# Gate and value products contracted over 32 inducing points in four row groups of TensorE, with a new token layout, load path and output path

## The chip, the cores and the metric

One core of one Trainium2 chip. The metric is device time in microseconds of one execution. Every kernel below was run next to the kernel before on the same chip. The kernel before scatters over 2.8% (1162 to 1195 us in all) at an unchanged mean TensorE clock of 0.985 to 0.995; runs over 1.5% above the fastest count as slow and are left out of the ratios. The **granted clock** is the share of TensorE's full clock that the profile's records show; in these runs it is 1.0 or 0.5 at any one time.

## The reference, cut to what matters

```python
B, N, m, C = 4, 12416, 32, 128            # x: (B, N, C), inducing: (m, C)
def mab(q, kv):                            # softmax attention, keys = values
    s = scale * (q @ kv.T);  s -= s.max(-1)
    a = exp(s);  a /= a.sum(-1) + 1e-9
    return a @ kv
h = mab(inducing, x)                       # "phase 1": 32 rows for each batch
z = mab(x, h)                              # 49664 tokens x 128
gate, val = relu(z @ w_gate), z @ w_val    # 128 -> 1536, each
out = (gate * val) @ w_out                 # 1536 -> 128
```

Each token's z is a mix of only 32 rows of h. So z @ w_gate = a @ (h @ w_gate), with h @ w_gate having 32 rows. The sum that divides the softmax can come out of the relu and out of the product. It then divides twice, at the very end.

## The kernel before

It works in blocks of 512 tokens, 24.25 blocks to a batch. `s2` is the score product of a block, `p2` its exponential, `zt` the block's z. The scores are [32 x 512], and z is made from them. Then come 12 feature tiles of 128, with a gate product, a value product, a relu on ScalarE, a multiply on VectorE and an output product each.

```python
for b in range(B):
    nc.gpsimd.dma_start(out=xh[b], in_=x[b])            # fp32 -> fp16 copy of x in DRAM
    for q in range(4):
        nc.sync.dma_start_transpose(out=xT[:, rows], in_=xh[b][rows])
    nc.sync.dma_start(out=x_sb[:, :, 0:C], in_=xh[b]...)
    ...                                                  # phase 1: s1, exp, h
    def stage_zt(j):
        nc.tensor.matmul(zT_ps, h16, p2[:, cols])        # z of the block
        nc.scalar.copy(out=zt, in_=zT_ps)
        ...                                              # z2c, reciprocal, its square
    def stage_ffn(G, ...):
        for i in range(NFF):                             # 12 feature tiles
            nc.tensor.matmul(g_ps, wg[:, i], zt)         # 128 rows contracted
            nc.tensor.matmul(v_ps, wv[:, i], zt)
            nc.scalar.activation(out=g16, in_=g_ps, func=AF.Relu, bias=zbias, scale=1.0)
            nc.vector.tensor_tensor(out=gv[:, i], in0=g16, in1=v_ps, op=ALU.mult)
            ...                                          # four tiles later:
            nc.tensor.matmul(outT_ps, wo[:, k], gv[:, k], start=(k == 0), ...)
        nc.scalar.copy(out=oT16, in_=outT_ps)
    ...   # later: 4 transposes on TensorE, 4 scalings on VectorE, store
```

PSUM is split by hand: 1 + 1 + 2 + 3 + 1 banks of 128 x 512 fp32.

The softmax here doesn't subtract the row's maximum and nothing guards it: scores larger than these inputs give would overflow.

## Time and profile before

| | before |
|---|---|
| time (3 runs) | 1177.48 us median, 1170.03 to 1189.86 |
| first gate product | 190.8 us |
| one block of 512 tokens | 9.47 us, of which TensorE needs 9.23 |

The page of the kernel before: its first line (busy us, share of the span, instructions), the granted TensorE clock in 40 slices of 29.4 us, the chain that ended last by engine, and two groups. A group line gives busy us and the mean ns of one, then the idle time before them with what ended most of it.

```profile
PE 986.6 (84%) x5357; PEld 426.7 (36%) x5357; DVE 844.2 (72%) x1803; ACT 913.0 (78%) x1606; POOL 5.0 (0%) x13
...
PEclk9999998999999999999999989999999999999999
...
PE 81%; SPq 12%; DMA 3%; ACT 2%; DVE 1%; issue 1%; POOL 0%; DVEq 0%; ACTq 0%; POOLq 0%
...
L273 DVE TENSOR_TENSOR gv<-g,v_ps 128x512 f16<-128x512 f16 (+1 forms) x1200 | 748.8, 665 | 94.9 <-PE v_ps L258 82.1
L266 ACT ACTIVATE g<-g_ps,zbias 128x512 f16<-128x512 f32 (+1 forms) x1200 | 742.5, 672 | 45.9 <-PE g_ps L251 39.9
```

The chain is TensorE for 81% and the SP queue for 12%. The latter is the transposing DMA that waits at the start. ScalarE hardly appears in the chain although its relus take 742 us: it keeps up. The waits of VectorE and ScalarE end with a product of TensorE.

### The profile page before, as it was taken

What the parts mean: (1) busy time and instruction counts of PE and PEld (TensorE: products, weight loads), DVE (VectorE), ACT (ScalarE), POOL (GpSimd) and SP (SyncE); (2) the same over time, 40 slices, a digit from 0 to 9 for tenths busy, and PEclk for the clock granted to TensorE, in tenths of its full rate; (3) what the DMA queues carried; (4) which work ended last, traced back from release to release, by engine and by line L of the source; (5) the groups of instructions that cost most, each with busy time, mean ns of one, the idle gap of its engine ahead of it and who ended that gap; (6) DMA issues with size and microseconds to landing.
All of it is one profiled execution on the core that took longest, in us unless ns stands there. A gap on an engine that the chain in (4) does not pass through costs nothing.

```text
span 1177.6 us, 16537 instructions
## 1 busy us (share of the span) xinstructions
PE 986.6 (84%) x5357; PEld 426.7 (36%) x5357; DVE 844.2 (72%) x1803; ACT 913.0 (78%) x1606; POOL 5.0 (0%) x13
## 2 busy tenths in 40 slices
PE   0000018999999999999999999999999999999998
PEld 0000014444444453444444444444444534444443
DVE  0000003999998948989999849998989489999987
ACT  0000025999999979999999879999999799999997
POOL 1000000000000000000000000000000000000000
PEclk9999998999999999999999989999999999999999
DMA  9999999000001443000000650011000000000001
GB/s 160 102 94 75 57 196 215 26 28 28 28 30 35 95 109 80 28 28 28 28 28 28 145 120 19 28 32 32 28 28 28 30 10 28 28 28 28 28 28 48
DMA packets 116472, 65.83 MB, mean 56 GB/s; under 512 B 53505, under 2 KB 115617, under 8 KB 115873
## 3 DMA queue, kind: packets, MB, share of 16 engines
q1 hardware_dynamic: 113968, 50.88, 25.3%
q0 software_dynamic: 2416, 13.89, 8.8%
q8 instruction: 42, 0.69, 0.3%
q14 instruction: 46, 0.37, 0.1%
HBM read 40.52 MB, written 38.14 MB: 67 GB/s over the span
## 4 chain that ended last, share of the span: by engine, by line
PE 81%; SPq 12%; DMA 3%; ACT 2%; DVE 1%; issue 1%; POOL 0%; DVEq 0%; ACTq 0%; POOLq 0%
PE g_ps L251 26%; PE v_ps L258 21%; PE outT_ps L287 14%; SPq L101 12%; PE outT_ps L295 7%; PE s_ps L165 3%; PE zT_ps L181 3%; PE h_ps L138 2%; PE z2c_ps L187 2%; PE ot_ps L216 2%; ACT g L266 2%; DMA xh_stage<-in_x_dram 1%; DMA x_sb<-xh_stage 1%; DVE gv L273 1%; PE s_psg L122 1%
## 5 line engine op out<-in xcount | busy, mean ns | idle before, releaser
L273 DVE TENSOR_TENSOR gv<-g,v_ps 128x512 f16<-128x512 f16 (+1 forms) x1200 | 748.8, 665 | 94.9 <-PE v_ps L258 82.1
L266 ACT ACTIVATE g<-g_ps,zbias 128x512 f16<-128x512 f32 (+1 forms) x1200 | 742.5, 672 | 45.9 <-PE g_ps L251 39.9
L258 PE MATMUL v_ps<-zt,wv 128*128 128x512 f16 (+1 forms) x1200 | 434.6, 376 | 0.3
L251 PE MATMUL g_ps<-zt,wg 128*128 128x512 f16 (+1 forms) x1200 | 426.9, 378 | 1.8
L287 PE MATMUL outT_ps<-gv,wo 128*128 128x512 f16 (+1 forms) x800 | 283.6, 374 | 0.8
L258 PEld LDWEIGHTS <-wv 128*128 128x128 f16 x1200 | 117.9, 98 | 103.6 <-issue 13.0
L251 PEld LDWEIGHTS <-wg 128*128 128x128 f16 x1200 | 106.5, 98 | 119.9 <-issue 43.1
L295 PE MATMUL outT_ps<-gv,wo 128*128 128x512 f16 (+1 forms) x400 | 148.1, 372 | 0.0
L146 DVE RECIPROCAL z1i<-h_ps 32x1 f32<-32x1 f32 x4 | 0.6, 156 | 205.3 <-PE h_ps L138 205.3
L122 PE MATMUL s_psg<-indT,xT 128*128 128x32 f16 x196 | 13.6, 181 | 156.0 <-DMA xT<-xh_stage 154.9
L129 ACT ACTIVATE p1T<-s_psg,zbias 128x128 f16<-128x128 f32 (+1 forms) x52 | 18.8, 367 | 161.1 <-PE s_psg L122 160.5
L217 DVE TENSOR_SCALAR osb<-ot_ps,z2isq 128x128 f32<-128x128 f16 x388 | 134.0, 345 | 10.8 <-PE ot_ps L216 8.8
L287 PEld LDWEIGHTS <-wo 128*128 128x128 f16 x800 | 77.9, 98 | 91.5 <-issue 4.2
L216 PE MATMUL ot_ps<-eye,oT 128*128 128x128 f16 x388 | 84.8, 219 | 1.4 <-DVE osb L217 1.3
L168 ACT ACTIVATE p<-s_ps,zbias 32x512 f16<-32x512 f32 (+1 forms) x100 | 66.3, 663 | 14.6 <-PE s_ps L165 4.6
L122 PEld LDWEIGHTS <-xT 128*128 128x128 f16 x388 | 16.0, 98 | 164.1 <-DMA xT<-xh_stage 157.3
L183 ACT CAST zt<-zT_ps 128x512 f16<-128x512 f32 (+1 forms) x100 | 58.3, 583 | 1.1 <-PE zT_ps L181 1.1
L216 PEld LDWEIGHTS <-oT 128*128 128x128 f16 x388 | 37.7, 97 | 56.4 <-issue 23.2
L303 ACT CAST oT<-outT_ps 128x512 f16<-128x512 f32 (+1 forms) x100 | 56.5, 565 | 0.9 <-PE outT_ps L295 0.9
L295 PEld LDWEIGHTS <-wo 128*128 128x128 f16 x400 | 38.9, 97 | 47.9 <-issue 12.9
L165 PE MATMUL s_ps<-xT,hT 128*32 128x512 f16 (+1 forms) x100 | 39.9, 399 | 5.4 <-ACT p L168 4.3
L138 PE MATMUL h_ps<-x_sb,p1T 128*32 128x129 f16 x388 | 32.4, 228 | 14.1 <-DMA x_sb<-xh_stage 14.1
(32 smaller groups left out, 213.0 us busy)
## 6 DMA issues: line engine op xcount, KB each, us to landing
out_dram<-osb SPq DMA_DIRECT2D x96, 256.0 KB, 2.3
xh_stage<-in_x_dram POOLq DMA_DIRECT2D x4, 3104.0 KB, 126.3
wg<-in_moe_w_gate_dram POOLq DMA_DIRECT2D x1, 384.0 KB, 18.6
wv<-in_moe_w_val_dram POOLq DMA_DIRECT2D x1, 384.0 KB, 19.9
wo<-in_moe_w_out_dram POOLq DMA_DIRECT2D x1, 384.0 KB, 107.1
xT<-xh_stage SPq DMA_TRANSPOSE x16, 6.2
out_dram<-osb SPq DMA_DIRECT2D x4, 64.0 KB, 1.7
x_sb<-xh_stage SPq DMA_DIRECT2D x4, 0.2 KB, 16.6
```

The source lines that it names most:

```text
L101: nc.sync.dma_start_transpose(out=xT[:, rows], in_=xh[b][rows])
L165: nc.tensor.matmul(s2_ps[:M, 0:BW], hT[:, 0:M], xT[:, cols], start=True, stop=True)
L168: nc.scalar.activation(out=p2[:, cols], in_=s2_ps[:M, 0:BW], func=AF.Exp, bias=zbias[:M], scale=sm_scale,)
L183: nc.scalar.copy(out=zt[:, 0:BW], in_=zT_ps[:, 0:BW])
L216: nc.tensor.transpose(dst, oT16[:, jj * P : (jj + 1) * P], eye)
L217: nc.vector.tensor_scalar(out=osb[:, jj, :], in0=dst, scalar1=z2isqs[j][:, jj : jj + 1], scalar2=None, op0=ALU.mult,)
L251: nc.tensor.matmul(g_ps[:, 0:BW], wg[:, i * P : (i + 1) * P], zt[:, 0:BW], start=True, stop=True,)
L258: nc.tensor.matmul(v_ps[:, 0:BW], wv[:, i * P : (i + 1) * P], zt[:, 0:BW], start=True, stop=True,)
L266: nc.scalar.activation(out=g16[:, 0:BW], in_=g_ps[:, 0:BW], func=AF.Relu, bias=zbias, scale=1.0,)
L273: nc.vector.tensor_tensor(out=gv[:, i, 0:BW], in0=g16[:, 0:BW], in1=v_ps[:, 0:BW], op=ALU.mult,)
L287: nc.tensor.matmul(outT_ps[:, 0:BW], wo[:, k, :], gv[:, k, 0:BW], start=(k == 0), stop=False,)
L295: nc.tensor.matmul(outT_ps[:, 0:BW], wo[:, k, :], gv[:, k, 0:BW], start=False, stop=(k == NFF - 1),)
```

## The change

The intent: take z out. Per batch, h @ w_gate and h @ w_val are computed once (`hgv`, laid out as four copies of 32 rows: gate, value, gate, value). The scores of two blocks are laid out in the same four groups of 32 partitions. The four products of a feature tile for two blocks then contract over 32 rows each, and each reads another 32 partitions, called a row group of the array below. Further: x is loaded as fp32 straight to SBUF with 97 neighbouring tokens to a partition; phase 1 of the next batch is spread over the present one; the output is transposed by DMA and scaled on GpSimd; all PSUM tiles come from one ring of eight banks; the order of instructions is written by hand.

```diff
-    ps_g = lambda s, d, n: ps("pG", 2, s, d, n)      (and four more pools)
+    def ring(name, shape=None, dtype=FP32):
+        return psum.tile(shape or [P, BLK], dtype, tag="ring", bufs=8, name=name)
...
-        nc.gpsimd.dma_start(out=xh[b], in_=x[b])
+    xv = [x[b].rearrange("(p t) c -> p t c", p=P) for b in range(B)]
+        nc.sync.dma_start(out=x32, in_=xv[b][:, t0:t1, :])
...
+                nc.tensor.matmul(ps[64 * k : 64 * k + 64, :], hT, xTs(xT, t0, TPB), ...)   # s2, k = 0, 1
+            nc.scalar.activation(out=p2, in_=ps, func=AF.Exp, scale=sm_scale)
...
-                nc.tensor.matmul(g_ps[:, 0:BW], wg[:, i * P : (i + 1) * P], zt[:, 0:BW], ...)
-                nc.tensor.matmul(v_ps[:, 0:BW], wv[:, i * P : (i + 1) * P], zt[:, 0:BW], ...)
-                nc.scalar.activation(out=g16[:, 0:BW], in_=g_ps[:, 0:BW], func=AF.Relu, bias=zbias, scale=1.0)
+                    for k in range(2):
+                        for j in range(2):
+                            ps = ring("gv_ps")
+                            r = 64 * k + 32 * j
+                            nc.tensor.matmul(ps, hgv[r : r + 32, s * P : (s + 1) * P], p2[r : r + 32, :], ...)
+                for f in fill.pop(at, []):       # s2, z2, s1 or h of another pair, by a table of slots
+                    f()
+                out_work(at, 2.0 if full else 1.0)   # two output products
+                for k in range(len(pss) // 2):
+                    nc.scalar.activation(out=g16, in_=pss[2 * k], func=AF.Relu)
+                    nc.vector.tensor_tensor(out=dst, in0=g16, in1=pss[2 * k + 1], op=ALU.mult)
+                    if k == 0:
+                        for f in todo:           # exps, casts, DMA issues, by the same table
+                            f()
...
+                ev_s2(b, pr, base + 6)           # s2 of the next pair goes into slot 6
+            def s1(q=q, at=at + 18): ...         # s1 of the next batch: slot 6 as well (18 = 12 + 6)
+                fill[at + 18].append(s1)
...
-                        nc.tensor.transpose(dst, oT16[:, jj * P : (jj + 1) * P], eye)
-                        nc.vector.tensor_scalar(out=osb[:, jj, :], in0=dst, scalar1=z2isqs[j]..., op0=ALU.mult)
+                nc.sync.dma_start_transpose(out=o16[:, 0:nt, :], in_=oT[:, 0:w])
+                        nc.gpsimd.tensor_scalar(out=osb[:, t, :], in0=o16[:, t, :], scalar1=zz, scalar2=zz,
+                                                op0=ALU.mult, op1=ALU.mult)
```

A **slot** below is a pair of blocks times one feature tile: four products, two relus, two multiplies, two output products. A pair has 12 slots, numbered 0 to 11.

## The prediction

> **What bounds the kernel now.** I read the page first (engine shares, the 40 slices), then the chain of work in order of time, then the timelines of TensorE, ScalarE and VectorE over one block of the steady part. The page's slices:
>
> ```profile
> PE   0000018999999999999999999999999999999998
> DVE  0000003999998948989999849998989489999987
> ACT  0000025999999979999999879999999799999997
> ```
>
> Each digit stands for 29.4 us. The reader is to see three things: six empty slices ahead, a dip at three places in the middle, and for the rest all three engines near full. So there are three separate accounts: the start, the three batch boundaries, the steady part. The start, from the chain in order of time:
>
> ```profile
> 1.26 17.64 DMA xh_stage<-in_x_dram
> 18.91 131.35 SPq L101
> ...
> 162.35 17.03 DMA x_sb<-xh_stage
> 179.42 7.07 PE h_ps L138 x97
> ...
> 190.79 0.54 PE g_ps L251
> ```
>
> The first batch of x is in DRAM as fp16 after 18.9 us, but its transposing DMA (L101) then sits in the queue for 131 us, behind the staging of the other batches and the weights; then x_sb is read, then h. The first gate product starts at 190.8 us. Nothing of that start is arithmetic. The steady part, from ScalarE's timeline (two exps of s2, L168, lie two blocks of 512 tokens apart):
>
> ```profile
> 362.83 0.68 ACT L168 ACTIVATE p<-s_ps,zbias 32x512 f16<-32x512 f32 x1
> 363.41 1.81 ACT L266 ACTIVATE g<-g_ps,zbias 128x512 f16<-128x512 f32 x3
> 365.12 0.58 ACT L303 CAST oT<-outT_ps 128x512 f16<-128x512 f32 x1
> 365.59 0.60 ACT L183 CAST zt<-zT_ps 128x512 f16<-128x512 f32 x1
> ...
> 381.77 0.68 ACT L168 ACTIVATE p<-s_ps,zbias 32x512 f16<-32x512 f32 x1
> ```
>
> 381.77 - 362.83 = 18.94, so 9.47 us a block. Starts also give the pace of each kind: three relus take 365.12 - 363.41 = 1.71, so 0.57 each; a cast is followed after 365.59 - 365.12 = 0.47. VectorE's and TensorE's timelines of the same stretch:
>
> ```profile
> 361.51 1.87 DVE L273 TENSOR_TENSOR gv<-g,v_ps 128x512 f16<-128x512 f16 x3
> ...
> 362.09 0.38 PE L295 MATMUL outT_ps<-gv,wo 128*128 128x512 f16 x1
> 362.40 0.39 PE L165 MATMUL s_ps<-xT,hT 128*32 128x512 f16 x1
> 362.72 0.61 PE L251 MATMUL g_ps<-zt,wg 128*128 128x512 f16 x2
> 363.17 0.38 PE L295 MATMUL outT_ps<-gv,wo 128*128 128x512 f16 x1
> 363.38 0.38 PE L258 MATMUL v_ps<-zt,wv 128*128 128x512 f16 x1
> 363.60 0.22 PE L216 MATMUL ot_ps<-eye,oT 128*128 128x128 f16 x1
> ...
> 367.10 0.38 PE L287 MATMUL outT_ps<-gv,wo 128*128 128x512 f16 x1
> 367.41 0.17 PE L187 MATMUL z2c_ps<-ones_m,p 32*128 32x1 f16 x1
> 367.51 0.39 PE L251 MATMUL g_ps<-zt,wg 128*128 128x512 f16 x1
> ```
>
> Three multiplies in 1.87 with the last lasting 0.68: (1.87 - 0.68)/2 = 0.597 each. Matmuls of one shape start 0.215 apart (363.17 to 363.38), whatever their printed 0.38. Where the shape changes from 128*128 the next starts 0.31 later, and back again 0.32 later, so one s2 product costs 0.63 - 0.215 = 0.41 and not 0.215. Adding up a block on TensorE: 36 x 0.215 = 7.74; s2 0.41; zT 0.40; the four z2c 0.44 (0.19 for one alone, 0.25 for the other three together); four output transposes at 0.06 = 0.24: 9.23 of the 9.47. TensorE is the bound. VectorE needs 12 x 0.597 + 4 x 0.27 (osb, start to start) + 0.3 = 8.5, ScalarE 12 x 0.57 + 0.58 + 2 x 0.47 = 8.4; both lie less than 12% below.
>
> Whole kernel: 190.8 + 97 blocks x 9.47 (918.6) + 6 after the last multiply leaves 62 for the three boundaries, some 20 each (s1, h and the first s2 of the next batch, where VectorE stands still).
>
> **What the Trainium skill says.** (1) "TensorE: Matmul & The Clock Gate", Part 3 (packing small matmuls): products contracted over 32 rows, placed in four row groups, run side by side; four of 512 columns measured 3.07 times as fast as in turn. Here no run shows it; all 32-row products of this kernel use one row group. (2) "TensorEngine Tiling (Array Packing)", Key Properties: a change of tiling mode drains the engine. The trace agrees: 0.31 and 0.32 against 0.215. (3) "ScalarE: Activation LUTs", What ACT_TABLE_LOAD costs: an activation with an immediate bias has about 93 ns less fixed cost than one whose bias is read from a [128,1] operand. The trace agrees: 685 ns with zbias against 577 and 596 for the casts, 0.57 against 0.47 between starts. (4) "SBUF — State Buffer", Who interferes with whom: VectorE with one SBUF input and outside its two-port modes does not contend with GpSimd. The multiply has one (g16; the other is PSUM), so the output scaling moved to GpSimd should not slow it. No run here shows it.
>
> **The change part by part.** The unit is a slot: for a pair of blocks one of the 12 feature tiles, so 4 products of 32 rows, 2 relus, 2 multiplies, 2 output products. There are 4 x (12 pairs x 12 + 1.5 for the remainder) = 582 slots.
>
> *TensorE, removed:* zT, the output transposes, and the 2 gate/value products of 128 rows per tile and block become 4 per slot side by side. *Cost now:* four starts some 0.04 apart (the trace's smallest spacing of load and product pairs: four s1 products in 0.27 with the last 0.177, so 0.03), then a mode change 0.32, the second output product 0.23 later, a mode change 0.31: 3 x 0.04 + 0.86 = 0.98. Per pair also two s2 (0.5), four z2 (0.3), a share of the next batch's s1 (0.4), h (8 products of 128 columns, 0.5) and the hgv products (0.3): 2.0/12 = 0.17. Sum 1.15 a slot, against 2 x 9.23/12 = 1.54 before.
>
> *VectorE, removed:* osb scaling and z2isq. *Stays:* 2 x 0.597 = 1.194, plus one reciprocal (0.18) and a little hgv per pair: 1.215.
>
> *ScalarE, removed:* the zt cast, half the exps (one for two blocks), and zbias; the diff gives no bias, which I take as an immediate. 24 x 0.475 + exp 0.48 + two oT 0.94 + half a phase-1 exp 0.3 + hgv 0.08 = 13.2 a pair, 1.10 a slot.
>
> So three engines lie at 1.15, 1.215 and 1.10: the bound moves from TensorE to VectorE. The floor is 582 x 1.215 = 707.
>
> *PSUM:* one ring of 8 banks. In a slot the first relu's bank is held about 1.1 us (product 0.39, handing over, relu 0.59), the first value bank 1.9, the second pair 1.6 and 2.5 (they wait for their turn): 7.1 bank-us in 1.215 is 5.8 banks, one more for the output sum, and now and then one for s2, z2, s1 or a second output sum. That is close to 8, so some slots begin late. I put the slot at 1.30, 7% over its floor: 757.
>
> *Start:* x comes as fp32 straight into SBUF. The trace read 6.4 MB in 17.6 us, so a chunk of 1 MB takes 3 us plus latency, the first is there at about 6. Per chunk there is a chain: cast (1.0), 8 transposes (0.6), copy out (1.0), s1 (0.6), exp (0.6), handings over 0.5: 4.3, times 6, plus 2 for the last tile: 34 us; then h, hgv, and the first pair, 4 to 8: 42 us for 190.8. *Boundaries:* phase 1 of the next batch is spread over the slots, all its DMA 12 slots ahead: 62 to about 0. *Tail:* output chain, cast, a transposing DMA (landed 4.9 to 6.2 us for 0.8 MB in the trace, so 2 to 3 for 128 KB), GpSimd scaling, store (2.3): 8 for 6.
>
> *Sum:* 42 + 757 + 8 = 807; I say 805. Of the 372 us won, about 149 come from the start, 62 from the boundaries, 162 from the steady part.
>
> **Rivals.** (a) *The row groups do not run side by side, or only in part.* For it: nothing here shows it happen, and each slot has two mode changes. At 0.215 apart the slot is 3 x 0.215 + 0.86 + 0.17 = 1.67, 582 x 1.67 + 50 = 1020: still faster, but TensorE-bound. At 0.1 apart: 1.33, some 840. Against: s1 pairs start 0.03 apart, so loads don't hold them up. (b) *The bank ring couples all three engines* and none is full: slot 1.40, 865. For it: my bank count. Against: the kernel before runs with 5 banks for gate and value and still lost only 0.24 of 9.47 a block. (c) *The output path becomes the wait.* SP's queue takes its work in order: transpose, wait for landing and for four GpSimd scalings, store, about 5 us of 7.8 a block, plus the next batch's transposes (3.7 us of queue time for 0.8 MB in the trace). If a transpose out of SBUF takes twice that or a scaling over 1 us, the rings of 3 for oT and o16 fill and ScalarE waits: 900 to 1000. Against: GpSimd and the DMA engines are nearly idle now (POOL 0 tenths, DMA 0 or 1 in the slices away from start and boundaries). (d) *The default bias is a pointer after all:* ScalarE 15.6 a pair, 1.30 a slot at full load; about 850.
>
> **Range and chances.** Below 755 VectorE would have to lose nothing (707 + 50 = 757), so 755 is the low end. The high end 890 takes in (b), (d), half of (a) and a start of 60 us. Start and boundaries alone are worth about 210 us, 18%, and don't rest on the row groups; so slower or same needs (c) in a bad form. Faster 0.97, same 0.02, slower 0.01.
>
> **What would show it.** Start: first relu of a gate tile near 42 us, no empty slices past the second. Boundaries: no dips in VectorE's digits. Steady: VectorE at 90% or more of the slot and the highest of the three; multiplies 0.597 apart in runs; relus about 590 ns, not 685. Row groups: four gv products starting 0.03 to 0.1 apart, each pair's tile groups followed by 0.3. Wrong if TensorE is in the chain for most of the steady part (a), if VectorE, ScalarE and TensorE are all under 90% with waits on each other for banks (b), or if ScalarE's cast of the output or SP's queue waits on landing and on GpSimd (c).

## The result, and the profile after

| | time, median | runs |
|---|---|---|
| before (4 runs of the same rounds) | 1182.14 us | 1170.03 to 1189.86 |
| after (4 runs) | 868.18 us | 861.98 to 874.37 |

The ratio is 0.7364, with a 95% interval of 0.7304 to 0.7424. A ratio here is the mean time of one kernel's fast runs over that of the other's fast runs of the same rounds, so it is not quite the ratio of the medians.

The page after. A slice is now 21.6 us:

```profile
PE 786.2 (91%) x4621; PEld 213.6 (25%) x4621; DVE 736.4 (85%) x1270; ACT 711.1 (82%) x1386; POOL 206.9 (24%) x418
...
DVE  3468888888998888897899888888699999999995
ACT  4658888887898888886889888887689988888885
...
PEclk9659999999999999998999999999699999999998
...
PE 56%; ACT 25%; DVE 9%; issue 9%; DMA 1%; POOL 0%; SPq 0%; POOLq 0%; ACTq 0%; DVEq 0%
...
L615 DVE TENSOR_TENSOR gv<-g,gv_ps 128x512 f16<-128x512 f16 x1152 | 710.7, 680 | 92.7 <-ACT g L610 88.8
L610 ACT ACTIVATE g<-gv_ps 128x512 f16<-128x512 f32 x1164 | 621.9, 610 | 125.3 <-PE gv_ps L584 117.9
...
L502 POOL TENSOR_SCALAR osb<-o,z2i 128x128 f32<-128x128 f16 x388 | 167.9, 447 | 620.6 <-DMA o<-oT 374.9
```

The empty slices ahead are gone. VectorE stands at 8 in most slices and reaches 9 throughout only in the last quarter, where no further phase 1 is due. Nobody owns the chain: TensorE 56%, ScalarE 25%, VectorE 9%. VectorE waits for ScalarE, ScalarE waits for TensorE. The clock line has dips in slices 1 and 2 and in slice 28 (counted from 0).

The start, from the chain of work in order of time (start us, us, what):

```profile
1.19 5.01 DMA x<-in_x_dram
...
11.00 0.94 ACT x L224
11.99 1.03 PE xT_ps L240 x8
...
36.66 1.02 ACT g L610 x2
```

The first chunk of x is there at 6.2 us, and each of six chunks then costs one round of about 4 us: cast (the second line's 0.94), transposes (1.03), sums, s1 and exp. The first relu of a gate tile starts at 36.7 us.

Now one pair in the middle. TensorE's timeline (start us, us, engine, line, operation, tiles, count, and in brackets the idle time before it):

```profile
305.50 0.51 PE L584 MATMUL gv_ps<-p,hgv 32*128 32x512 f16 x4
305.94 0.41 PE L164 MATMUL s_ps<-xT,hT 128*64 128x512 f16 x2
306.57 0.40 PE L359 MATMUL s1T_ps<-xT,indT 128*32 128x512 f16 x4 [0.22 <-ACT g L610]
...
307.44 0.39 PE L584 MATMUL gv_ps<-p,hgv 32*128 32x512 f16 x4
```

Four products of 32 rows take 0.51 and 0.39 us together, where one takes 0.37 to 0.39: the row groups do run side by side. Between the two groups lie the two s2 and the four s1 products, with a wait of 0.22 us for a relu to free a bank, so the second group comes 1.94 us after the first. Where nothing holds TensorE up, a slot takes it 0.87 us, from one group of four to the next:

```profile
443.13 0.40 PE L584 MATMUL gv_ps<-p,hgv 32*128 32x512 f16 x4
443.46 0.60 PE L480 MATMUL o_ps<-gv,wo 128*128 128x512 f16 x2
444.00 0.75 PE L584 MATMUL gv_ps<-p,hgv 32*128 32x512 f16 x4
```

The four start within 0.01 us of each other here; the prediction had 0.12 for that, and so 0.98 for the slot. ScalarE's timeline of the first place:

```profile
307.86 0.60 ACT L610 ACTIVATE g<-gv_ps 128x512 f16<-128x512 f32 x1 [0.85 <-PE gv_ps L584]
308.35 0.59 ACT L174 ACTIVATE p<-s_ps 128x512 f16<-128x512 f32 x1
308.83 0.60 ACT L369 ACTIVATE p1T<-s1T_ps 128x512 f16<-128x512 f32 x1
309.31 0.21 ACT L369 ACTIVATION_READ_ACCUMULATOR p1T<-s1T_ps 128x1 f32 x1
309.40 0.60 ACT L491 CAST oT<-o_ps 128x512 f16<-128x512 f32 x1
309.86 2.59 ACT L610 ACTIVATE g<-gv_ps 128x512 f16<-128x512 f32 x5
...
325.39 0.59 ACT L174 ACTIVATE p<-s_ps 128x512 f16<-128x512 f32 x1
```

Between the relu at 307.86 and the next at 309.86 ScalarE does four other things in a row. And ahead of it ScalarE stood idle for 0.85 us. VectorE pays for both:

```profile
308.49 0.69 DVE L615 TENSOR_TENSOR gv<-g,gv_ps 128x512 f16<-128x512 f16 x1 [0.66 <-ACT g L610]
310.53 3.68 DVE L615 TENSOR_TENSOR gv<-g,gv_ps 128x512 f16<-128x512 f16 x6 [1.35 <-ACT g L610]
...
314.24 4.82 DVE L615 TENSOR_TENSOR gv<-g,gv_ps 128x512 f16<-128x512 f16 x8
```

It stands idle for 0.66 + 1.35 us around one multiply, and then runs six and eight multiplies without a gap. From the starts of every second multiply in the trace I worked out the length of each slot (medians; the first row is of pairs 2 to 6); this is not a view of the profile:

```
after, us per slot     slot 0    1    2    3    4    5    6    7    8    9   10   11    pair
pair with s1 due         1.20 1.20 1.50 1.30 1.20 1.20 1.94 2.64 1.20 1.20 1.27 1.20   17.03
pair of last batch       1.20 1.20 1.50 1.20 1.20 1.20 1.44 2.07 1.20 1.20 1.27 1.20   15.84
```

Most slots are exactly 1.20 us, which is two multiplies 0.60 apart. Of 576 slots 319 lie at 1.22 or less. The whole excess over 1.20 is 117.5 us, and 86 slots longer than 1.60 us hold 87.5 of it. So the account of the profiled 864.2 us is:

| part | predicted | in the trace |
|---|---|---|
| start, to the first multiply | 42 | 37.2 |
| slots of full pairs, 576 | 749 (1.30 each) | 808.7 (1.404 each) |
| the four remainders of 128 tokens | 8 (6 slots of 1.30) | 7.3 |
| after the start of the last multiply | 8 | 11.0 |
| sum | 807 | 864.2 |

Against the 1177.6 us of the kernel before (190.8 to the first gate product, about 981 in blocks and boundaries, 6 after) this is 154 us won at the start, 165 in blocks and boundaries, and 5 lost at the end.

The excess of 117.5 by place: the two cold pairs at the start 12.0; the fifteen pairs 2 to 6 of the first three batches 39.5 (2.6 each); pairs 8 and 9 of these batches, where h of the next batch is summed and `hgv` made, 32.3; the last batch, which has no phase 1 beside it, 15.8; the rest 18.

The two cold pairs show in the windows of the trace (stretch, length, busy us and count of PE, PEld, DVE, ACT, POOL, then granted clock, DMA share, GB/s):

```profile
40.00:60.00 20.00, 17.33 (x63) 3.63 (x59) 15.09 (x27) 12.44 (x23) 0.00 (x0) 0.50 0.19 59
...
300.00:320.00 20.00, 18.16 (x96) 4.60 (x94) 17.54 (x31) 16.95 (x35) 5.30 (x9) 1.00 0.59 170
```

At clock 0.50 TensorE gets 63 products done in 20 us where it does 96 later, while it is shown as 87% busy. The records give clock 0.5 from 29.8 to 67.4 us, and again for 3.4, 6.8 and 17.1 us at 200, 402 and 603 us, each time in pair 8 or 9 of a batch, so they add to the excess there.

The tail, from the timeline of all engines:

```profile
855.20 0.94 ACT L491 CAST oT<-o_ps 128x512 f16<-128x512 f32 x2 [1.64 <-PE o_ps L480]
...
858.45 1.14 SPq L495 DMA_TRANSPOSE o<-oT  x1
...
860.88 0.45 POOL L502 TENSOR_SCALAR osb<-o,z2i 128x128 f32<-128x128 f16 x1 [0.74 <-DMA o<-oT]
```

After the last cast ends (856.1) three outputs pass one after the other through transposing DMA, GpSimd and the store on one queue, until 864.2.

### The profile page after: what moved, and what is told of

It is laid out like the page before. It is cut to its first block, busy times and chain, and to the rows that moved or that the text cites. A ratio compares the mean times of both kernels' runs of the same rounds, so it can differ in the third digit from the quotient of the medians.

```text
span 864.2 us, 14829 instructions
## 1 busy us (share of the span) xinstructions
PE 786.2 (91%) x4621; PEld 213.6 (25%) x4621; DVE 736.4 (85%) x1270; ACT 711.1 (82%) x1386; POOL 206.9 (24%) x418
## 4 chain that ended last, share of the span: by engine, by line
PE 56%; ACT 25%; DVE 9%; issue 9%; DMA 1%; POOL 0%; SPq 0%; POOLq 0%; ACTq 0%; DVEq 0%
PE gv_ps L584 27%; PE o_ps L480 22%; ACT g L610 16%; DVE gv L615 8%; ACT oT L491 3%; ACT p L174 2%; ACT p1T L369 1%; PE z_ps L183 1%; PE s_ps L164 1%; PE s1T_ps L359 1%; PE h_ps L425 1%; PE xT_ps L240 1%; PE hgv_ps L140 1%; DMA x<-in_x_dram 1%; ACT x L224 1%
## 5 line engine op out<-in xcount | busy, mean ns | idle before, releaser
L615 DVE TENSOR_TENSOR gv<-g,gv_ps 128x512 f16<-128x512 f16 x1152 | 710.7, 680 | 92.7 <-ACT g L610 88.8
L610 ACT ACTIVATE g<-gv_ps 128x512 f16<-128x512 f32 x1164 | 621.9, 610 | 125.3 <-PE gv_ps L584 117.9
L584 PE MATMUL gv_ps<-p,hgv 32*128 32x512 f16 x2304 | 429.8, 391 | 35.3 <-ACT g L610 9.8
L480 PE MATMUL o_ps<-gv,wo 128*128 128x512 f16 x1152 | 359.0, 393 | 13.0 <-ACT g L610 11.7
L502 POOL TENSOR_SCALAR osb<-o,z2i 128x128 f32<-128x128 f16 x388 | 167.9, 447 | 620.6 <-DMA o<-oT 374.9
L584 PEld LDWEIGHTS <-hgv 32*128 32x128 f16 x2304 | 98.1, 91 | 318.1 <-issue 296.2
L480 PEld LDWEIGHTS <-wo 128*128 128x128 f16 x1200 | 76.3, 98 | 230.7 <-issue 220.5
L491 ACT CAST oT<-o_ps 128x512 f16<-128x512 f32 (+1 forms) x100 | 57.4, 574 | 1.7 <-PE o_ps L480 1.6
L339 POOL CAST x<-x 128x2048 f16<-128x2048 f32 x18 | 34.0, 1890 | 5.3 <-DMA x<-in_x_dram 2.1
L174 ACT ACTIVATE p<-s_ps 128x512 f16<-128x512 f32 x48 | 28.4, 592 | 2.6 <-PE s_ps L164 2.6
```

Of the source, the lines that this page charges most:

```text
L174: nc.scalar.activation(out=p2, in_=ps, func=AF.Exp, scale=sm_scale)
L339: nc.gpsimd.tensor_copy(out=s["x16"][:, t0:t1, :], in_=s["x32", q])
L480: nc.tensor.matmul(c["ps"][:, 0:w], wo[:, i, :], c["gv"](i), start=(i == 0), stop=(i == NFF - 1))
L491: nc.scalar.copy(out=oT[:, 0:w], in_=ps[:, 0:w])
L502: nc.gpsimd.tensor_scalar(out=osb[:, t, :], in0=o16[:, t, :], scalar1=zz, scalar2=zz, op0=ALU.mult, op1=ALU.mult,)
L584: nc.tensor.matmul(ps, hgv[r : r + 32, s * P : (s + 1) * P], p2[r : r + 32, :], start=True, stop=True,)
```

## The experiments

Three theories about the missing 117.5 us, and two about the rest:

- **LUMP.** The table of slots puts s2 and s1 both in slot 6; their exps and the cast of an output sum then all fall in slot 7. Each of these is an eviction: an instruction that reads a finished product out of PSUM. So ScalarE has exp, exp, accumulator read and cast in a row between two relus, and VectorE runs dry.
- **BANKS.** The ring of eight banks is too small for what is in flight there, whatever the order on ScalarE. This is rival (b) of the prediction.
- **VectorE as the bound.** Ordinary slots are 1.20 us because of two multiplies and nothing else, and the slow slots are slow because VectorE is still behind.
- **Output path.** Rival (c): SP's queue and GpSimd hold up the oT and o16 buffers.
- **Clock.** The cold pairs are slow because of the granted clock, not because of work that is missing.

Unless another kernel is named, diffs are against the kernel after. Changed lines only.

### e1_spread: s2 and s1 in different slots

```diff
-                ev_s2(b, pr, base + 6)
+                ev_s2(b, pr, base + 3)
-            def s1(q=q, at=at + 18):
+            def s1(q=q, at=at + 22):
-                fill[at + 18].append(s1)
+                fill[at + 22].append(s1)
```

> Three small pieces of work are moved, nothing is added or left out: the s2 product of the next pair from slot 6 of a pair to slot 3 (its exp from slot 7 to 4), and the s1 product of the next batch from slot 6 to slot 10 (its exp from slot 7 to 11). In the changed kernel most slots take 1.20 us, VectorE's two multiplies, but slots 6 and 7 of a pair take 1.94 and 2.64, since in slot 7 ScalarE does both exps and the output cast between two relus. Theory LUMP (these evictions in a row starve VectorE): pairs with s1 fall from 17.04 to about 15.3 us, pairs without from 15.84 to about 15.2, the whole to about 820 us, ratio to the kernel before about 0.70. Rival BANKS (the eight PSUM banks couple all slots, wherever the work lies): within 1% of 866 us. Rival EVEN (VectorE is the bound everywhere and the rest is noise): no change.

Measured: 832.32 us median (826.85 to 835.18), ratio to before 0.7084 (0.7028 to 0.7140). Pairs with s1 went from 17.03 to 15.88, pairs of the last batch from 15.84 to 15.10. The excess over 1.20 fell from 117.5 to 85.4 us. ScalarE's timeline of the pair now reads:

```profile
288.39 0.60 ACT L610 ACTIVATE g<-gv_ps 128x512 f16<-128x512 f32 x1 [0.64 <-PE gv_ps L584]
288.88 0.59 ACT L369 ACTIVATE p1T<-s1T_ps 128x512 f16<-128x512 f32 x1
289.36 0.20 ACT L369 ACTIVATION_READ_ACCUMULATOR p1T<-s1T_ps 128x1 f32 x1
289.45 2.55 ACT L610 ACTIVATE g<-gv_ps 128x512 f16<-128x512 f32 x5
...
295.72 0.59 ACT L174 ACTIVATE p<-s_ps 128x512 f16<-128x512 f32 x1
```

The run is 12 us above the 820 expected, and far from what BANKS (within 1% of 866) and EVEN (no change) said. The exp of s1 is alone between its relus, and that of s2 comes 6.8 us later. Where the evictions were drawn apart the long slot disappeared: no slot of the ordinary pairs 2 to 6 is over 1.67 any more (2.64 in the kernel after), and slots 6 and 7 are at 1.20 and 1.22. What remains over 1.3 is slots 2, 4 and 11 with one eviction each (1.44, 1.58, 1.67), and slots 3 and 10 with the products of s2 and s1 (1.34, 1.46). The place of a few instructions was worth 4% of the time. Whether it is ScalarE's order or the products and their banks this run can't say, as both moved.

### e2_late_exp: the products stay, the exps move

```diff
-            post[at + 1].append(act)                     # exp of s2
+            post[at + (1 if pr == NPAIR else 2 if pr == 0 else 3)].append(act)
-                ev_z2(b, pr, base + 9)
+                ev_z2(b, pr, base + 10)
-                post[at + 1].append(act)                 # exp of s1
+                post[at + 5].append(act)
-                    post[at + 2].append(tr)              # its transposing DMA
+                    post[at + 6].append(tr)
```

> The s2 and s1 products stay in slot 6, but their exps come later on ScalarE: the exp of s2 in slot 9, that of s1 in slot 11, so that only the output cast is left in slot 7. The price is that the two PSUM banks are held 2 and 4 slots longer. Theory LUMP (ScalarE's evictions in a row starve VectorE): most of the gain of moving both, 820 to 840 us. Rival BANKS (free PSUM banks are what is short): no gain or slower, 866 to 900 us. Rival TensorE (the time that the two products take on TensorE in slot 6, about 1.2 us with their mode changes, is what is lost): little gain, 855 to 866 us.

Measured: 845.80 us (845.44 to 845.91), ratio 0.7204 (0.7158 to 0.7250). Pairs with s1 16.46, of the last batch 15.28, excess 96.5 us. This leaves the products of s2 and s1 in slot 6 and holds their two banks longer than before, which by BANKS alone makes it worse (z2 moves one slot later along with the exp). It became better, so the row of evictions does cost time. But 845.8 lies between the range of LUMP (820 to 840) and that of the rival TensorE (855 to 866): of the 1.15 us that e1 won per pair with s1 only 0.57 came, and of the 0.74 of the last batch 0.56. By slots the remainder lies in 6 to 8, which take 1.50, 1.58 and 1.31 in pairs with s1, where e1 has 1.20, 1.22 and 1.20. There TensorE makes the two products and their banks are then held; which of the two costs the time stays open.

### e6_seven_banks: one bank fewer

```diff
-        return psum.tile(shape or [P, BLK], dtype, tag="ring", bufs=8, name=name)
+        return psum.tile(shape or [P, BLK], dtype, tag="ring", bufs=7, name=name)
```

> The ring of PSUM tiles gets 7 buffers instead of 8. My count in the prediction was 5.8 banks for gate and value, one for the output sum, now and then one more. Theory BANKS (there is no bank to run ahead with, so each engine's late start is passed on): ordinary slots rise above 1.20, to 1.3 or more, and the whole by 5% or more: 910 to 960. Theory LUMP alone: ordinary slots stay at 1.20 and only the slow ones grow, 870 to 890.

Measured: 946.70 us (940.85 to 957.33), ratio 0.7978 (0.7933 to 0.8024). The profiled run counts as slow, so from it I use only the last batch, which ran at full clock: a pair there takes 16.50 instead of 15.84, 0.66 more. By slots, 1, 3 and 10 grew (to 1.43, 1.31 and 1.41, from 1.20, 1.20 and 1.27) and 2 a little, but the long slots 6 and 7 did not (1.47 and 2.07 for 1.44 and 2.07), and 0, 4, 5 and 8 stayed at 1.20. So with seven banks the ring is a bound too, in other slots than the long ones; the time is in the range of BANKS, but ordinary slots did not all rise, as it said they would. The other runs, at a mean clock of 0.871 to 0.885, count as fast and are the ones in the ratio. In 48 pairs that would be 32 us (an estimate from these two lengths) of the 78 lost; the larger part goes with the clock, which now fell again and again:

```profile
PEclk9559766796999776679599879778789999999998
```

In that run the records give clock 0.5 for 290 us in all, in stretches of 3.4 to 47.8 us, where the kernel after had 72. The ring couples the engines, and with one bank less the clock is lost far more often; that pauses of TensorE cause this is only argued from the two appearing together. BANKS does not explain slots 6 and 7. A larger ring was not tried.

### e3_half_mult: VectorE's work halved

```diff
-                            gv=(lambda i, g=gvs[k]: g[:, i, :]),
+                            gv=(lambda i, g=gvs[k]: g[:, i, 0 : BLK // 2].unsqueeze(1).to_broadcast([P, 2, BLK // 2])),
-                    nc.vector.tensor_tensor(out=dst, in0=g16, in1=pss[2 * k + 1], op=ALU.mult)
+                    nc.vector.tensor_tensor(out=dst[:, 0:cw], in0=g16[:, 0:cw], in1=pss[2 * k + 1][:, 0:cw], op=ALU.mult)
```

with cw = 256 for full pairs. It multiplies only half of the tokens and feeds that half twice to the output product, so it computes something else. The comparison with the reference still passed, presumably because with scores this small the outputs of neighbouring tokens are nearly alike.

> Wrong result on purpose: each multiply of VectorE takes 256 of the 512 columns, and the output products read those 256 twice, so TensorE and ScalarE have the same work. If VectorE sets the pace in the ordinary slots, as predicted, they fall from 1.20 us to what TensorE or ScalarE needs, 0.95 to 1.05, and the whole to 760 to 800 us (420 or so of the 582 slots times 0.2). If the banks or ScalarE set the pace, less than 2%: 850 us or more.

Measured: 793.58 us (791.62 to 796.66), ratio 0.6762 (0.6715 to 0.6809).

```profile
PE 743.0 (93%) x4621; PEld 207.4 (26%) x4621; DVE 511.8 (64%) x1270; ACT 702.3 (88%) x1386; POOL 207.9 (26%) x418
```

```profile
728.49 4.05 ACT L610 ACTIVATE g<-gv_ps 128x512 f16<-128x512 f32 x8
```

Slots 0, 3, 4, 5 and 8 fell to 0.98 us, from 1.20 (slot 3 of pairs with s1 from 1.30). So VectorE is their bound. The next one is ScalarE: in such slots it runs relu after relu without idle time (the line above), 0.49 apart, which is 0.98 for two. TensorE's own 0.87 lies below that. But of the 319 slots at 1.22 or less only 188 fell below 1.05; slots 1, 9 and 11 stay at 1.15 to 1.21, so for them this run does not show that VectorE alone is the bound. Slots 6 and 7 stay at 1.78 and 2.53 (1.94 and 2.64 after), although VectorE has little to do. They are not VectorE's.

### e4_zbias: the relu's bias as an operand again

```diff
-                    nc.scalar.activation(out=g16, in_=pss[2 * k], func=AF.Relu)
+                    nc.scalar.activation(out=g16, in_=pss[2 * k], func=AF.Relu, bias=zbias, scale=1.0)
```

> One part undone: the relus read their bias from the [128,1] tile of zeros again. From the kernel before, a relu then takes 0.57 us between starts and not 0.48, so 24 of them 2.3 us more a pair. If ScalarE were the bound: 48.5 pairs x 2.3 = 110 us more, 975. Theory LUMP: in ordinary slots 2 x 0.57 = 1.14 stays under VectorE's 1.20, but ScalarE recovers more slowly after a row of other evictions: 15 to 45 us more, 880 to 910. If VectorE were the bound everywhere: no change.

Measured: 915.79 us (913.03 to 916.27), ratio 0.7793 (0.7731 to 0.7855).

```profile
L612 ACT ACTIVATE g<-gv_ps,zbias 128x512 f16<-128x512 f32 x1164 | 715.9, 701 | 80.9 <-PE gv_ps L586 76.3
```

A relu takes 701 ns instead of 610, 91 more, where the prediction quotes 93. So in the kernel after the bias is not read as an operand, and rival (d) is out. Ordinary slots stay at 1.20, as two relus still fit. The long ones grow: pairs with s1 to 17.65, of the last batch to 16.75, excess 167 us for 117.5. It came out 6 us above the top of the range. Clock 0.5 lasted 132 us for 72, which I had not counted.

### b1_imm_bias: the same in the kernel before

```diff
                     func=AF.Relu,
-                    bias=zbias,
-                    scale=1.0,
```

> The kernel before, with only the bias of the gate relus left out, so that ScalarE's relus shrink from 685 to about 600 ns and start 0.48 apart, ScalarE from 8.4 to 7.3 us a block. If TensorE set the pace of the kernel before (9.23 of 9.47 us a block), nothing: within 1%, 1170 to 1185 us. If ScalarE did: up to 97 x 1.1 = 105 us less.

Measured: 1194.53 us (1174.36 to 1205.14), against 1181.85 for the kernel before on that chip. Only one of its four runs counts as fast (1174.36), so there is no ratio; the profiled run is a slow one too, yet its clock is 0.989.

```profile
L266 ACT ACTIVATE g<-g_ps 128x512 f16<-128x512 f32 (+1 forms) x1200 | 657.3, 584 | 86.4 <-PE g_ps L251 37.1
```

The relus are 88 ns shorter (672 to 584), ScalarE's busy time fell from 913.0 to 828.6 us, and there is no sign of a gain. The kernel before was not bound by ScalarE: its faster relu only waits longer for g_ps (86.4 for 45.9). That it was bound by TensorE, and not by VectorE, rests on the chain (81%) and on what the two waited for, not on this run. The same edit is worth some 50 us in the kernel after (e4: 0.7793 - 0.7364 of about 1180) and nothing here.

### e5_one_group: all products in one row group

```diff
-                            r = 64 * k + 32 * j
+                            r = 0
```

Wrong: all four products take group 0.

> Wrong result on purpose: all four gate and value products of a slot read rows 0 to 31 of hgv and p2, so they share one row group and cannot run side by side; counts, shapes, banks and mode changes stay. If the row groups are what lets TensorE get out of the way, the four start 0.215 us apart, TensorE needs 0.98 + 3 x 0.18 = 1.5 us for a slot instead of 0.98, and the whole takes 582 x 1.5 + 50 plus the small work = 950 to 1040 us, TensorE the bound. Rival (four products of 32 rows run one after another anyway): no change, 866.

Measured: 1719.89 us (two runs, 0.1 us apart), ratio 1.4525 (1.4440 to 1.4609). The page, and one line of TensorE's timeline:

```profile
PE 1694.8 (99%) x4621; PEld 370.1 (22%) x4621; DVE 823.0 (48%) x1270; ACT 787.9 (46%) x1386; POOL 208.3 (12%) x418
...
PEclk7555555555555555555555555555555555555555
```

```profile
400.04 1.88 PE L584 MATMUL gv_ps<-p,hgv 32*128 32x512 f16 x4
```

Four products take 1.88 us: they run in turn. The clock was 0.5 from 21.6 to 1707.7 us, so the fair comparison is with the cold pairs of the kernel after, at the same clock:

```profile
62.80 0.61 PE L584 MATMUL gv_ps<-p,hgv 32*128 32x512 f16 x4
```

There four take 0.61 us, a third of it, and the next four follow after 1.51 us, where a slot here takes 2.78. That settles the row groups. But I missed the time by far, because of that clock, with TensorE busy for 99% of the run. At full clock the slot would take about 1.5 us (an estimate: the undisturbed 0.87, and three starts 0.215 apart, the pace of the kernel before), which is what the expectation said; the prediction's rival (a) had 1.67, with 0.17 of small work in it.

### e7_pool_twice: every GpSimd scaling done twice

```diff
-                    for t in range(nt):
+                    for t in list(range(nt)) * 2:
```

> Each scaling of the output on GpSimd is done twice (the same values written to the same place): 1.73 us more GpSimd work per block, and the chain from transposed output to store that much longer. Rival (c) of the prediction (the output path is a wait): 20 us or more longer. My reading of the trace (GpSimd waits 375 us for landings and is 24% busy): under 1%, plus up to 2 us in the tail. If GpSimd and VectorE disturbed each other in SBUF, the multiplies would also grow from 680 ns.

Measured: 870.17 us (862.62 to 874.86), ratio 0.7343 (0.7287 to 0.7399): the same as the kernel after.

```profile
PE 780.7 (91%) x4621; PEld 214.8 (25%) x4621; DVE 736.2 (86%) x1270; ACT 711.1 (83%) x1386; POOL 375.9 (44%) x806
```

GpSimd was busy 376 us for 207, and pairs stayed at 17.03 and 15.84. The output path is off the chain, and rival (c) is out. VectorE's busy time did not change either (736.2 for 736.4), so twice the GpSimd work did not slow its multiplies, as point (4) of the prediction said.

### e8_warm: idle products that keep TensorE at work at the start

```diff
+    def warm(n, w, m):
+        ps = ring("warm_ps")
+        for _ in range(n):
+            nc.tensor.matmul(ps, w, m, start=True, stop=True)
...
     for q in range(NCH):
+        if q > 4:
+            warm(4, ones16, x16[:, 0:TPB, :])
...
     first_h(NCH - 1)
+    warm(10, ones16, x16[:, 0:TPB, :])
...
+                if at < NFF:
+                    warm(2 if at < 2 else 1, wg[:, 0:P], wg[:, 0:BLK])
                 out_work(at, 2.0 if full else 1.0)
```

> The changed kernel with idle products added on TensorE, 128 rows by 512 columns, read by nothing: 4 each while the sixth and seventh tiles of x are cast, 10 while h of the first batch is normalised, and 1 or 2 in each of the first 12 slots. In the changed kernel the clock granted to TensorE is 0.5 from 29.8 to 67.4 us, and those pairs take 20.4 us and not 17.0. The run with one row group sat at 0.5 for all of its 1718 us with TensorE busy 99%[...]. Theory CLOCK: the first two pairs keep a clock of 1.0 and fall to about 17.5 us each, 5 to 7 us less in all: 857 to 862 us, ratio about 0.729. Rival (the clock falls for the idle time around 33 us alone, and extra products in the slots only cost): 5 us or more slower.

Measured: 859.01 us (851.42 to 859.49), ratio 0.7313 (0.7258 to 0.7367). The intervals of this ratio and of the kernel after overlap. The pairs in the trace are clearer: the first two took 14.89 and 16.41 us for 20.38 and 20.41, 9.5 us less together.

```profile
40.00:60.00 20.00, 19.52 (x110) 5.21 (x108) 19.56 (x36) 17.74 (x34) 2.56 (x5) 1.00 0.28 80
```

The clock in this stretch is 1.00 for 0.50, and VectorE does 36 operations for 27. More products made the start faster, against the rival that they only cost: the cold pairs were the clock's doing. Later low stretches (3.4, 17.1 and 17.1 us at 191, 389 and 597 us) remained.

### e9_all: e1 and e8 together, products ordered gate, gate, value, value

The edits of e1_spread and e8_warm, and:

```diff
-                    for k in range(2):
-                        for j in range(2):
+                    for j in range(2):
+                        for k in range(2):
```

with the four banks handed on in the old order.

> Candidate for a better version: s2 and s1 moved as in the run that spread them, the idle products of the warm start, and in each slot both gate products ahead of both value products, since ScalarE needs the gate products first and VectorE needs the value products last. The move alone gave 832 us. With theory CLOCK 5 to 7 us less; the order should help where only two or three banks are free, some 0.1 to 0.3 us a pair: 815 to 825 us in all. Rival: the order delays the first value product and VectorE with it, 832 or more.

Measured: 820.06 us (817.23 to 820.85), ratio 0.6996 (0.6959 to 0.7033). It is correct and the best version: by the ratios 0.6996 / 0.7364 = 0.95 of the kernel after.

```profile
PEclk9999999999999999999999999999799999999998
```

Pairs of the last batch take 15.10 us, as in e1, so the order of the four products gave nothing. What it has over e1 is the clock: the first two pairs took 15.08 and 15.76 us for 19.22 and 20.00. In pairs 8 and 9 of the first two batches the clock stayed full as well; they took 17.97 and 17.68 us, and in the third batch, with 13.7 us at half clock, 18.45 and 21.06. The excess over 1.20 us is 68.3 us.

### b2_one_stage: the kernel before, with one batch staged

```diff
-        nc.gpsimd.dma_start(out=xh[b], in_=x[b])
+        if b == 0:
+            nc.gpsimd.dma_start(out=xh[0], in_=x[0])
-            nc.sync.dma_start_transpose(out=xT[:, rows], in_=xh[b][rows])
+            nc.sync.dma_start_transpose(out=xT[:, rows], in_=xh[0][rows])
-            out=x_sb[:, :, 0:C], in_=xh[b].rearrange("(t p) c -> p t c", p=P)
+            out=x_sb[:, :, 0:C], in_=xh[0].rearrange("(t p) c -> p t c", p=P)
```

Wrong: all four batches read batch 0. It takes away the staging of the other three, which stood in the way of the first transposes, and nothing of the arithmetic.

> The kernel before, wrong on purpose: only the first batch of x is staged in DRAM, and all four batches read it. All compute stays. If the start of 190 us was the transposing DMAs queued behind the staging of the other three batches and the weights, as the prediction says, the first gate product comes at 60 to 80 us and the whole takes 110 to 130 us less, about 1050 to 1070. If the transposes from DRAM are slow by themselves: no change in the start.

Measured: 1055.68 us (1052.99 and 1058.36), ratio 0.9010 (0.8900 to 0.9119). The chain of work in order of time:

```profile
18.80 8.41 SPq L102
...
39.23 16.86 DMA x_sb<-xh_stage
...
68.42 0.54 PE g_ps L252
```

The transposes start at the same time as before and are through after 20 us, where the first alone sat in the queue for 131. The first gate product comes at 68.4 us, not 190.8. These 122 us are the whole gain of the run: 116 between the means of the fast runs, 126 between the two profiled ones. So most of the start was a queue behind other copies.

## Why the prediction was right, and where it was off

The measured 868 us lie inside the predicted range (805, from 755 to 890), on its slow side, and the kernel is faster, as said at 0.97. By the prediction's own steps:

- **TensorE bounds the kernel before.** Right as far as shown: b1 shortened the relus by 88 ns and won nothing, so ScalarE is out; for VectorE it rests on the trace.
- **Start, 42 us.** Right in kind and slightly too long: 37.2. Of the 149 us counted as won here, b2 shows 122 as pure waiting for other copies.
- **Boundaries, 62 to about 0.** Half right. No empty stretch is left, and the three remainders in the middle take 2.03 us each. But a dip to 6 is left in VectorE's digits, in slice 28. Summing h and making `hgv` moved into pairs 8 and 9, and there the excess is 32 us, some 16 more than six other pairs with s1 have (6 x 2.6). Most of it is likely work and not the low clock: with the clock full, e9 still has 6.9 us over 1.20 a slot in these two pairs of a batch, and 13.7 us of half clock adds some 4.
- **The row groups run side by side.** Right (0.61 us for four, against 1.88 in turn in e5 at the same clock). Rival (a) is out. The 0.98 for the products of a slot was too long: TensorE needs 0.87 undisturbed. (The 840 of rival (a) is a slip of addition too: 582 x 1.33 + 50 is 824.)
- **The floor, 1.215 us a slot, from VectorE.** Right: 1.20, two multiplies 0.60 apart, in over half of all slots, and e3 shows VectorE as the bound in 188 of those 319. ScalarE is closer behind than the 0.475 a relu said: 0.49 apart in a row.
- **No pointer for the bias, relu about 590 ns.** Right: 610 on average, 701 with the operand. Rival (d) is out. Had it been true it would have cost more than the 850 said: e4 has 916.
- **The slot at 1.30, from counting banks.** This is the mis-sized term. It measured 1.404, and 576 slots make 60 us of it, more than the whole 57 by which the sum of 807 fell short of the profile's 864. The working averaged the engines over a pair and took a small loss spread over all slots. In fact most slots lose nothing, and 86 lose 87.5 us. In the long slots 6 and 7 evictions in a row on ScalarE make about half of the loss that e1 took away (e2; in the last batch three quarters); the other half goes with the two products in slot 6, by TensorE's time or by their banks. Drawing them apart won 32 of the 117.5 us of excess (e1), and the clock at the start makes 9.5 more (e8). Rival (b) gave 865 by a slot of 1.40 and so had the number, and "all under 90% with waits on each other" is what the shares came to near enough (VectorE 85%, where the prediction asked for 90% or more; ScalarE 82%; but TensorE 91%). As a mechanism it is not shown for the long slots, which one bank fewer left as they were (e6); that its number fits is luck at least in part.
- **The clock** was in no step. Cold pairs cost 9.5 us at the start (e8), and the low stretches at the batch ends are part of the 32.
- **Tail, 8 us.** It took 11: three outputs go through transpose, GpSimd and store one after another.

What stays open: how the remainder in e9_all, 68 us over 1.20 a slot, divides between single evictions, banks and TensorE's own changes of shape. And what in TensorE's work lets the clock fall at the batch ends.

## What to carry to other kernels

Where three engines lie within a fifth of each other, add up each slot of the schedule by itself and not the average of a loop: short evictions and products crowded into one slot cost more than the same spread over several, and moving two numbers in the table won 4%. Shorten an operation only where the chain waits for it: the same 90 ns off a relu was worth some 50 us in one of these kernels and nothing in the other. Read the clock line next to the busy line, since an engine can be 99% busy at half its clock.

## What the Trainium skill lacked or had wrong

- "TensorE: Matmul & The Clock Gate", Part 1 (The HAM clock gate), says that the clock follows how busy TensorE has been, in windows of 3413 ns, and is full after about 3.4 us of sustained work. The low stretches here fit the window in length (3.4, 6.8, 13.7, 17.1 us). But e5_one_group stayed at 0.5 for 1686 us on end with TensorE 99% busy on products of which two in three used 32 of 128 rows. Busy time alone does not raise the clock. What is counted instead the page does not say and no run here shows.
- The same part describes a clock that falls when a kernel cycles through PSUM banks with pauses. The runs are consistent with it, though none shows the cause, and give a size: eight banks to seven took the time at half clock from 72 to 290 us (profiled runs, the second a slow one; the mean clock of the fast runs went from 0.946 to 0.965 down to 0.871 to 0.885).
- "TensorE: Matmul & The Clock Gate", Part 3, gives 3.07 times for four row groups. The runs agree: at half clock four products took 0.61 us side by side and 1.88 in turn, 3.1 times. No page has a time for a slot that alternates packed and full products, with its changes of mode: 0.87 us here at full clock for four packed and two full ones, of which some 0.32 and 0.31 lie at the two changes.
- "DMA: Bandwidth & Descriptors", DMA Transpose (X-bar), has no time for a small transpose within SBUF (elsewhere the page has a bandwidth alone). Here 128 KB took 1.14 us in the queue and landed after 2.4 us.
